# One PV pass moved ahead of the scores after six query groups, and query banks taken by halves

## The chip, the cores, the metric

One core of a Trainium2 chip. The time is the device time of one execution in microseconds (us). Each comparison runs two kernels on the same chip in alternating rounds; a ratio is the mean time of one kernel's fast runs over the mean of the other's fast runs of the same rounds, so it is not quite the ratio of the medians quoted beside it. The span of a profile is one profiled execution from its first to its last instruction, about 1.8 us less than its time.

## The reference, cut to what matters

```python
xn = layernorm(x)                                   # x: 2048 x 448
q  = (xn @ wq)          # 16 query heads of 256;  keys and values: 8 heads, the last 512 positions
p  = softmax(q @ k.T / 16)                          # per head 2048 x 512
s  = (p @ v, heads side by side) @ wo               # 2048 x 448
g  = silu((gelu(xn @ w_gate) * (xn @ w_up)) @ w_down)
out = x + s * g
```

## The kernel before

The kernel handles the feed-forward part first, then attention in 64 *steps*: 4 blocks of 512 rows times 16 query heads. Step m multiplies queries with keys (`s_mm`, "scores", eight passes of the matmul engine PE), takes exponentials on ScalarE (ACT), normalises on VectorE (DVE) and transposes the probabilities by DMA into `pT`. PV, the product with the values (`pv`, eight passes), follows two steps later (`LAG = 2`), so that PE has other work while a step's softmax and transpose run. Queries are made for up to eight steps at once, in query groups that start at steps 0, 4, 12, 18, 26, 34, 42, 50 and 58.

```python
def q_group(n, pairs, more_act=False):     # queries of two heads, into two pairs of banks
    ...
    group(units, 0, QC, True, True)        # 28 passes of 64 rows (two at a time: rows 0-63, rows 64-127)
    for i, b in enumerate(pairs):          # copied out by ScalarE (first half) and VectorE (second half)
        act(qT[:, s, 0, :], bank[b], ACT.Copy, (b_ps[b],), (b_qT[s][0],))
        K.op("dve", lambda v, s=s, b=b: v.tensor_copy(qT[:, s, 1, :], bank[b + 1]), ...)

def pv(m):
    h = m % Hq
    g, x = h // 2, m % NPT                 # g: key/value head, used by two query heads
    for e in range(2):
        b = BB[m % 2 * 2 + e]
        mms([(bank[b]..., va[:, g, j, e * P:(e + 1) * P], pT[:, x, ...], j == 0, j == NJ - 1)
             for j in range(NJ)], [b_va[g]] + b_pT[x], (b_ps[b],))     # NJ = 4, so 8 passes in all
        ...                                # copied out to oT

for m in range(NS):                        # cut to the order on PE
    if m in groups:
        for i in range(m, hi, 2):
            p = (i - m) // 2
            q_group(i, ((cur, nxt[::-1], (cur[1], nxt[1])) if three else (cur, nxt) * 2)[p], end)
            ...
            if m == Q0 + QS and p == 0:    # the third group, step 12
                for g in range(6, Hkv):
                    load_k(g)              # DMA transposes on the SP queue
                for g in range(5, Hkv):
                    load_v(g)              # plain loads on the same queue
    s_mm(m)
    ...
    if len(late) == LAG:
        pv(late.pop(0))
    ...
    late.append(m)
```

A bank is a stretch of the memory that PE writes its results to. `cur` and `nxt` are two bank pairs each: scores use the four banks of `cur` (`AB`), PV those of `nxt` (`BB`).

The softmax here doesn't subtract the row's maximum and nothing guards it: scores larger than these inputs give would overflow.

## Time and profile before

| | before |
|---|---|
| time, median of the first three runs | 540.66 us (540.63 to 542.68) |
| span of the profile | 540.2 us |
| PE busy | 533.2 us (99%) |
| all waits of PE that the profile names | 3.4 us |
| third query group's start to first score pass of step 13 | 13.00 us (187.16 to 200.16) |

Columns of the waits: the waiting engine and its line, what released it, then total us, times, longest. A row of the timeline: start in us, length in us, engine, line, operation, output<-inputs, shape, count; in brackets the idle time before it and its releaser. PEld is PE's weight load, L394 the helper through which nearly all matmuls go. Tiles tell the kinds: bank<-xnT,wq are queries, bank<-kT,qT scores, bank<-pT,va PV. The lines stand in the prediction. One more answer of the same trace, for the three value loads at step 12 (issue to landing):

```profile
L379 SPq DMA_DIRECT2D va<-in_A_v_cache_dram x3: 502/580/583, 192.1 to 193.3; - x3
...
DMA to landing us min/median/max: 6.3/6.3/7.5
```

The first of the three, key head 5, was issued at 192.12 and landed 6.26 us later, at 198.38.

### The profile page before, as it was taken

How to read it: one execution, taken by the hardware profiler on the slowest of the kernel's cores; microseconds unless marked ns; L12 is line 12 of the kernel's file. 1: busy time of each engine (PE TensorE's matmuls, PEld its weight loads, DVE VectorE, ACT ScalarE, POOL GpSimd, SP SyncE). 2: the span in 40 equal slices, each digit the busy share in tenths (PEclk: the TensorE clock that was granted, in tenths of full speed). 3: DMA queues.
4: the chain of work that ended last, by engine and by line, in shares of the span. 5: the costliest groups of instructions: out<-in, count | busy, mean ns of one | idle time of the engine just before them, and what ended most of it. 6: DMA issues, size and time to landing. Idle time of an engine off the chain costs nothing.

```text
span 540.2 us, 10920 instructions
## 1 busy us (share of the span) xinstructions
PE 533.2 (99%) x4155; PEld 310.6 (58%) x4180; DVE 383.6 (71%) x839; ACT 314.2 (58%) x782; POOL 39.7 (7%) x78
## 2 busy tenths in 40 slices
PE   9999999999999999999999999999999999999998
PEld 5556656459644444984444469544444884444487
DVE  6689886798767757934875786367667934776785
ACT  5466355873568768116866850488488106876820
POOL 1131120000000010003001000120000003001010
PEclk9999999999999999999999999999999999999999
DMA  9569173932598686302861860067448302872821
GB/s 296 123 187 108 53 126 87 282 70 60 112 171 138 156 190 147 59 1 82 167 141 50 152 137 1 18 156 139 96 106 146 72 1 69 164 157 73 149 66 35
DMA packets 171604, 61.38 MB, mean 114 GB/s; under 512 B 155104, under 2 KB 168416, under 8 KB 171552
## 3 DMA queue, kind: packets, MB, share of 16 engines
q1 hardware_dynamic: 167488, 51.30, 45.0%
q0 software_dynamic: 3008, 8.72, 6.9%
q8 instruction: 33, 0.54, 0.4%
q10 hardware_dynamic: 1056, 0.66, 0.4%
q14 instruction: 19, 0.16, 0.1%
HBM read 19.76 MB, written 3.67 MB: 43 GB/s over the span
## 4 chain that ended last, share of the span: by engine, by line
PE 87%; ACT 4%; DMA 4%; DVE 3%; issue 1%; SPq 1%; ACTq 0%; DVEq 0%
PE bank L394 86%; ACT p L830 4%; DMA pT<-pn 2%; DVE pn L837 2%; DMA va<-in_A_v_cache_dram 1%; PE bank L511 1%; DVE rden L834 1%; SPq L382 1%; PE bank L492 0%; DVE oTh L855 0%; ACT oTh L385 0%; DVE xnT L884 0%; DVE gl L424 0%; DVE xnT L388 0%; DVE epst L425 0%
## 5 line engine op out<-in xcount | busy, mean ns | idle before, releaser
L830 ACT ACTIVATE p<-bank 128x512 f32<-128x512 f32 x256 | 150.6, 596 | 28.9 <-DVE pn L837 26.5
L394 PE MATMUL bank<-pT,va 128*128 128x512 bf16 x512 | 120.9, 379 | 0.8 <-DMA pT<-pn 0.5
L394 PE MATMUL bank<-kT,qT 128*128 128x512 bf16 x487 | 117.8, 379 | 2.3 <-ACT qT L385 1.0
L837 DVE TENSOR_SCALAR pn<-p,rden 128x512 bf16<-128x512 f32 x256 | 112.9, 483 | 8.7 <-DMA pT<-pn 4.4
L394 PE MATMUL bank<-xnT,wq 64*128 64x512 bf16 x768 | 94.9, 376 | 0.0
L394 PEld LDWEIGHTS bank<-pT,va 128*128 128x128 bf16 x512 | 49.4, 98 | 62.5 <-DMA pT<-pn 3.2
L394 PEld LDWEIGHTS bank<-kT,qT 128*128 128x128 bf16 x512 | 49.3, 98 | 61.7 <-issue 3.4
L394 PE MATMUL bank<-xnT,wgu 64*128 64x512 bf16 (+2 forms) x768 | 83.9, 350 | 0.1
L385 ACT ACTIVATE qT<-bank 128x512 bf16<-128x512 f32 x76 | 44.1, 596 | 51.6 <-PE bank L394 50.0
L815 DVE CAST qT<-bank 128x512 bf16<-128x512 f32 x52 | 34.8, 690 | 49.4 <-PE bank L394 49.4
L394 PEld LDWEIGHTS bank<-xnT,wq 64*128 64x128 bf16 x768 | 36.7, 94 | 46.3 <-ACT p L830 1.7
L394 PEld LDWEIGHTS bank<-xnT,wgu 64*128 64x128 bf16 x768 | 37.6, 94 | 36.0 <-issue 0.5
L834 DVE RECIPROCAL rden<-rsum 128x2 f32<-128x2 f32 x128 | 21.1, 165 | 48.3 <-ACT p L830 48.2
L830 ACT ACTIVATION_READ_ACCUMULATOR p<-bank 128x1 f32 x256 | 51.6, 202 | 0.0
L394 PE MATMUL bank<-wt,sr 128*128 128x224 f16 x512 | 50.0, 259 | 0.0
L394 PEld LDWEIGHTS bank<-wt,sr 128*128 128x128 f16 x512 | 49.0, 98 | 0.4 <-ACT oTh L385 0.2
L385 ACT ACTIVATE gl<-bank 128x512 bf16<-128x512 f32 x56 | 33.0, 596 | 26.4 <-PE bank L394 22.1
L560 DVE TENSOR_TENSOR actTh<-bank,gl 128x512 f16<-128x512 f32 x56 | 37.4, 688 | 11.3 <-PE bank L394 5.8
L855 DVE TENSOR_SCALAR oTh<-bank 128x512 f16<-128x512 f32 x62 | 42.3, 683 | 0.0
L385 ACT ACTIVATE oTh<-bank 128x512 f16<-128x512 f32 x66 | 38.9, 590 | 3.8 <-PE bank L394 3.8
L394 PE MATMUL bank<-wt,oTh 128*128 128x224 f16 (+1 forms) x416 | 38.4, 252 | 0.0
L394 PEld LDWEIGHTS bank<-wt,oTh 128*128 128x128 f16 x416 | 37.2, 98 | 0.9
(77 smaller groups left out, 387.8 us busy)
## 6 DMA issues: line engine op xcount, KB each, us to landing
wtb<-in_A_wo_dram POOLq DMA_DIRECT2D x4, 896.0 KB, 10.8
wq<-in_A_wq_dram SPq DMA_DIRECT2D x2, 1536.0 KB, 7.9
va<-in_A_v_cache_dram SPq DMA_DIRECT2D x8, 256.0 KB, 6.3
pT<-pn SPq DMA_TRANSPOSE x128, 2.8
xr<-in_A_x_dram POOLq DMA_DIRECT2D x15, 112.0 KB, 2.3
wd<-in_B_w_down_dram SPq DMA_DIRECT2D x1, 1568.0 KB, 7.5
g<-g_all POOLq DMA_DIRECT2D x14, 112.0 KB, 2.3
out_dram<-xr POOLq DMA_DIRECT2D x12, 112.0 KB, 2.1
```

The lines of the kernel that those rows point to most:

```text
L382: K.op("sp", lambda e, o=o, i=i: e.dma_start_transpose(o, i), reads, writes, dma=True)
L385: K.op("act", lambda e, o=o, i=i: e.activation(o, i, func, scale=scale), reads, writes)
L394: ins = e.matmul(o, lhsT=l, rhs=r, start=st, stop=sp, skip_group_check=True)
L511: ins = e.matmul(bank[b][:, 0:w], lhsT=gl[:, 0, 0:P], rhs=gl[:, 0, 0:w], start=True, stop=True)
L560: K.op("dve", lambda e: e.tensor_tensor(actTh[:, c % 2, f, :], bank[b + 1], gl[:, s, :], ALU.mult), (b_ps[b + 1], b_gl[s]), (b_actT[c % 2] ...
L815: K.op("dve", lambda v, s=s, b=b: v.tensor_copy(qT[:, s, 1, :], bank[b + 1]), (b_ps[b + 1],), (b_qT[s][1],))
L830: K.op("act", lambda e, b=b, r=r, z=z: e.activation(p32[:, z, :], bank[b], ACT.Exp, scale=att_scale, accum_out=rsum[:, r:r + 1]), (b_ps[b] ...
L834: K.op("dve", lambda e, r=r: e.reciprocal(rden[:, r - 1:r + 1], rsum[:, r - 1:r + 1]), b_rsum[r - 1:r + 1], b_rden[r - 1:r + 1])
L837: K.op("dve", lambda e, r=r - 1 + t, z=(n - 1 + t) % NP32, y=y, t=t: e.tensor_scalar(pn[:, y, t, :], p32[:, z, :], rden[:, r:r + 1], None, ...
L855: K.op("dve", lambda v, i=i, b=b: v.tensor_scalar(oTh[:, i, :], bank[b], WS, None, op0=ALU.mult), (b_ps[b],), (b_oT[i],))
```

## The change

Its intent: after a query group, scores seem to wait for ScalarE's last query copies. One PV pass of the head two steps back is put between, as cover. PV's bank must be free by then, so in the groups of four query pairs (26, 34, 42, 50) the last two pairs each take one half of both bank sets (`cur[0], nxt[0]`, then `cur[1], nxt[1]`) instead of a whole set. The groups of three pairs (12, 58) keep their bank order. The early pass comes in six groups: steps 12, 26, 34, 42, 50 and 58.

```diff
-        def pv(m):
+        def pv(m, part=None):
...
-                     for j in range(NJ)], [b_va[g]] + b_pT[x], (b_ps[b],))
+                     for j in range(NJ) if part is None or (part == 0) == (e == j == 0)], [b_va[g]] + b_pT[x], (b_ps[b],))
+                if part == 0:
+                    break
...
         for m in range(NS):
+            split = m in groups and m not in (0, Q0, Hq + LAG)
...
-                    q_group(i, ((cur, nxt[::-1], (cur[1], nxt[1])) if three else (cur, nxt) * 2)[p], end)
+                    q_group(i, ((cur, nxt[::-1], (cur[1], nxt[1])) if three else (cur, nxt, (cur[0], nxt[0]), (cur[1], nxt[1])) if split else (cur, nxt) * 2)[p], end)
...
+            if split:
+                pv(late[0], 0)
             s_mm(m)
...
-                pv(late.pop(0))
+                pv(late.pop(0), 1 if split else None)
```

## The prediction

> **What bounds the kernel now.** I read the page first: the busy shares, the slices and the queues.
>
> ```profile
> span 540.2 us, 10920 instructions
> PE 533.2 (99%) x4155; PEld 310.6 (58%) x4180; DVE 383.6 (71%) x839; ACT 314.2 (58%) x782; POOL 39.7 (7%) x78
> PEclk9999999999999999999999999999999999999999
> ```
>
> The matmul engine (PE) is busy 99% of the span at the full clock in all 40 slices, and no other engine is above 71%. A busy PE is not a PE at its peak, though, so what can be won is in the spacing of its instructions. Next I read the waits of PE, the whole list:
>
> ```profile
> PE bank L511 <- DVE epst L425: 1.2, 1, 1.2
> PE bank L394 <- ACT qT L385: 1.0, 6, 0.2
> PE bank L394 <- issue: 0.5, 3, 0.2
> PE bank L394 <- DMA pT<-pn: 0.5, 2, 0.3
> PE bank L394 <- DMA va<-in_A_v_cache_dram: 0.2, 1, 0.2
> ```
>
> All its waits together come to 3.4 us. The line that the change seems aimed at is the second: six waits before the scores (bank<-kT,qT), put down to ScalarE's copy of the queries (ACT qT), 0.2 us each. Before believing it I looked at the timeline of PE and of its weight loads (PEld) around two of the places where queries (bank<-xnT,wq) give way to scores. The first is the third query group, ahead of head step 12:
>
> ```profile
> 194.94 1.46 PE L394 MATMUL bank<-xnT,wq 64*128 64x512 bf16 x12
> 196.56 1.67 PE L394 MATMUL bank<-kT,qT 128*128 128x512 bf16 x7 [0.16 <-issue]
> 198.42 1.90 PE L394 MATMUL bank<-pT,va 128*128 128x512 bf16 x8 [0.19 <-DMA va<-in_A_v_cache_dram]
> 200.16 1.89 PE L394 MATMUL bank<-kT,qT 128*128 128x512 bf16 x8
> ...
> 196.33 1.41 PEld L394 LDWEIGHTS bank<-kT,qT 128*128 128x128 bf16 x8 [0.42 <-issue]
> 198.42 1.41 PEld L394 LDWEIGHTS bank<-pT,va 128*128 128x128 bf16 x8 [0.69 <-DMA va<-in_A_v_cache_dram]
> ```
>
> The second is the group ahead of step 26, with the copies of the last query pair beside it:
>
> ```profile
> 289.72 1.46 PE L394 MATMUL bank<-xnT,wq 64*128 64x512 bf16 x12
> 290.57 1.25 ACT L385 ACTIVATE qT<-bank 128x512 bf16<-128x512 f32 x2 [1.78 <-PE bank L394]
> 291.11 1.41 PEld L394 LDWEIGHTS bank<-kT,qT 128*128 128x128 bf16 x8 [0.42 <-issue]
> 291.33 1.67 PE L394 MATMUL bank<-kT,qT 128*128 128x512 bf16 x7 [0.16 <-ACT qT L385]
> 292.85 1.89 PE L394 MATMUL bank<-pT,va 128*128 128x512 bf16 x8
> ```
>
> Three readings. (1) A 512-column pass takes 0.216 us start to start: eight take 200.16 - 198.42 = 1.73. Scores show "x7" although eight weights are loaded, and 292.85 - 291.33 = 1.52 is room for seven: the first score pass's record is missing. It began 0.216 earlier, at 196.34 and 291.12, with the weight loads. The 64-row query passes run in pairs, 0.216 a pair: twelve from 194.94 end their slots at 196.24, from 289.72 at 291.01. So the real hole before scores is about 0.10 us, not 0.16 plus. (2) The hole is the same where the profile names no releaser (step 12) and where it names ScalarE (step 26). The scores of step 26 use queries of the group's first pair and a bank of its third, copied more than 2 us before; the last pair's copies end at 291.82, after the scores began. So ScalarE did not end this wait. (3) At step 12 the PV pass had a real wait: it started 198.42 when its eight score passes had ended at 198.07, because the values of its key head had only then landed.
>
> **What the Trainium skill says.** "TensorEngine Tiling (Array Packing)", Key Properties: "Changing tiling mode (not just tile) drains the TensorE". "TensorE: Matmul & The Clock Gate", section "Step-by-step: what each phase is for", adds that a weight load is pulled ahead of running matmuls only where row groups don't conflict or it goes to the background buffer. The trace agrees: query passes use 64 rows (64*128), scores and PV 128 (128*128), every such switch costs about 0.10 us in either direction, and a 128-row to 128-row change (scores to PV at 292.85) costs none. The other direction:
>
> ```profile
> 277.09 1.89 PE L394 MATMUL bank<-pT,va 128*128 128x512 bf16 x8
> 278.92 0.82 PE L394 MATMUL bank<-xnT,wq 64*128 64x512 bf16 x6
> ```
>
> Eight passes from 277.09 end at 278.82; the next starts 278.92. The same page, Part 1 ("The HAM clock gate"), says that the clock falls to half after an idle window of some 3.4 us. No stall in this trace is long enough to show that.
>
> **The change part by part.** *Work.* Nothing is added or removed: order of instructions shows equal counts on DVE, ACT and SP in the same order. On PE, at the six groups before steps 12, 26, 34, 42, 50 and 58, one of the eight PV passes of the head two steps back moves ahead of the eight score passes; seven stay behind them. 16 x 0.216 = 3.45 us per step as before.
>
> *Banks by halves.* In the four-pair groups (26, 34, 42, 50) the third pair takes the front halves of both bank sets and the fourth the back halves, so the bank of the early PV pass was freed a pair ago. Scores 5 to 8 now use banks that the last pair filled. The first of these is finished three pairs (0.65 us) before the group's end; its copies start 0.44 before the end (290.57 against 291.01) and take 0.60 on ScalarE and 0.69 on VectorE, so they end at +0.16 and +0.25. Scores want those banks at 0.10 + 0.22 + 4 x 0.216 = +1.18 and +1.61. Margin 0.9 us: no wait. In the third pair the second bank half is wanted four slots (0.86) after the second pair's end and is free at +0.25. No wait either. Cost 0.
>
> *The hole.* The first 128-row pass after the queries is now PV instead of scores. It is still a switch from 64 to 128 rows with nothing loaded ahead. I expect the 0.10 us to stay in all six: gain 0.
>
> *Step 12.* Here the early PV pass belongs to step 10 and reads the values of key head 5. These are loaded by the SP queue behind the last transposes of the steps before and two key loads, all unchanged:
>
> ```profile
> 188.74 0.65 SPq L382
> 189.43 1.30 SPq L382
> 190.78 1.29 SPq L382
> 192.12 6.26 DMA va<-in_A_v_cache_dram
> 198.38 0.05 issue
> ```
>
> They land at 198.38 whatever PE does in between: every item of this chain is issued before PE leaves the query group. Before, the eight score passes (1.73 us) lay in that time and only 0.35 us was left over. After, PE meets the wait with the first pass at 196.24 and stands until 198.42. Then come one PV pass (to 198.64), eight scores (to 200.37) and seven PV (to 201.88). Before, this point was reached at 200.16. Cost +1.72 us. PE is the bound for the rest of the program, so nothing gives it back.
>
> *The later exponentials.* Scores come 0.22 us later at the other five groups, so softmax and its transposed tile (pT) for the first head do too, while the PV pass that needs them starts at the same time as before. By the landing times in the trace that slack is about 1.18 us at steps 26, 42 and 58 and falls to about 0.97. At 34 and 50, after a projection, it is only 0.04, but there ScalarE is held by a third query copy: its first exponential starts about 1.09 us after the scores' weights instead of 0.65, and 0.22 + 0.65 = 0.87 is still under that. Cost 0, at most 0.2 each.
>
> Sum: 0 + 0 + 1.72 + 0 = +1.7 us, 540.66 + 1.7 = 542.4.
>
> **The rivals.** *A: the intent works.* If the six waits are ScalarE's after all, or if PV weights can be loaded under 64-row passes where the query weights cannot, 0.10 us goes at each of five groups; with no wait at step 12 also there: 6 x 0.10 = 0.6, giving 540.1. Only the releaser column speaks for it; the equal hole at step 12 and at the switches the other way speak against. A mixed result (five holes closed, step 12 delayed) is 540.66 + 1.72 - 0.5 = 541.9. *B: the values land earlier.* Were the load tied to something the change moves, the loss would shrink. With no traffic moved I see nothing; the load took 6.26 us against 6.3 as the median of its kind, so it is not an outlier either. *C: the clock.* PE would stand for 2.2 us at step 12. That is under the 3.4 us of the page, but close; half a clock for one window would cost about 1.7 us more (an estimate from that page): 544.1. *D: late pT.* Waits of 0.3 us for a late transpose already occur at single heads (landings take 2.8 in the median, 4.7 at most); other phases may move a few, either way by some tenths.
>
> **Range and chances.** Step 12 is nearly certain in sign; its size depends on the landing, which may vary by a few tenths between runs. The three times of before are 540.63, 540.66 and 542.68, so one execution in three was 2 us longer by itself. I predict 542.4 us, 541.2 to 543.7 in 8 of 10. A 2% change is 10.8 us, over five times the largest effect I can name: faster 0.01, same 0.985, slower 0.005.
>
> **What would show it right or wrong.** Right: in the waits of PE the wait for va rises from 0.2 to about 2 us, sitting before one single PV pass ahead of step 12's scores, and step 13's scores start about 1.7 us later than 200.16. The small waits at the other five groups stay at about 0.16, now in front of a PV pass. Scores 5 to 8 after a group run at 0.216 spacing. PEclk stays 9 in the slice. Wrong: no long wait for va (the load lands before 196.3), five holes gone (rival A), score passes waiting for ScalarE or VectorE copies (my bank margin was wrong), or slowed passes after the stall (rival C).

## The result

The changed kernel took 542.33 us in the median of six runs (540.95 to 544.06), the kernel before 541.25 in the median of its six (540.63 to 542.68). The ratio is 1.0019, 95% interval 0.9997 to 1.0041: the same by the 2% measure, a mean of 1.0 us more, and by these runs alone not even clear of zero. Both spread over 2 to 3 us, so the traces must carry the argument. The page of the changed kernel and its list of PE's waits:

```profile
span 540.4 us, 10915 instructions
PE 533.0 (99%) x4155; PEld 311.2 (58%) x4180; DVE 383.5 (71%) x839; ACT 314.5 (58%) x782; POOL 39.7 (7%) x78
...
PEclk9999999999999999999999999999999999999999
```
```profile
PE bank L394 <- issue: 1.4, 2, 1.2
PE bank L511 <- DVE epst L425: 1.2, 1, 1.2
PE bank L492 <- DVE xn L467: 0.4, 1, 0.4
PE bank L394 <- ACT qT L385: 0.3, 2, 0.2
PE bank L394 <- DMA pT<-pn: 0.2, 1, 0.2
```

Six ACT qT waits became two. The two stand at steps 4 and 18, which the change leaves alone; the four that went stood at 26, 34, 42 and 50. The sum of that line fell by 0.7 us, yet nothing got shorter, as the groups below show. New is a wait of 1.2 us put down to "issue", that is to nothing the profile shows. PE's timeline says where, and the sequencer's own instructions (source line L153, the semaphore waits) say what:

```profile
194.40 1.46 PE L394 MATMUL bank<-xnT,wq 64*128 64x512 bf16 x12
197.11 0.38 PE L394 MATMUL bank<-pT,va 128*128 128x512 bf16 x1 [1.25 <-issue]
197.54 1.67 PE L394 MATMUL bank<-kT,qT 128*128 128x512 bf16 x7
199.05 1.67 PE L394 MATMUL bank<-pT,va 128*128 128x512 bf16 x7
200.56 1.89 PE L394 MATMUL bank<-kT,qT 128*128 128x512 bf16 x8
```
```profile
L153 PEldq EVENT_SEMAPHORE  x1: 2413/2413/2413, 194.6 to 194.6; - x1
```
```profile
L379 SPq DMA_DIRECT2D va<-in_A_v_cache_dram x3: 503/507/580, 191.6 to 192.8; - x3
...
DMA to landing us min/median/max: 5.4/5.5/7.0
```

The queries end their slots at 195.70. The PV pass starts at 197.11, alone, then eight scores (the first record is missing), then the other seven PV passes. PE's sequencer stood in one semaphore wait of 2413 ns from 194.64 to 197.06. The first value load was issued at 191.58 and took 5.44, so it landed at 197.02: the load ended the wait. In the kept trace that instruction names two semaphores, and the load is seen there directly: one belongs to the transposed tile and was last raised at 187.53, the other is the one that this load raises, last at 197.02. The profile names "issue" because the wait sits in an instruction of the sequencer ahead of the weight load and the weight load itself names another semaphore, satisfied at 195.86. "Perfetto Trace Analysis", section "Identifying Dependency Chains", says that an instruction which waits on several engines may have such EventSemaphore instructions ahead of it; this trace agrees, with that one instruction.

The start of the third group to step 13's scores took 200.56 - 186.62 = 13.94 us, 0.94 more than before. The spans differ by only 0.2. The rest is chance: waits of PV for late transposes elsewhere, counted from the weight loads, came to some 1.3 us in the trace of before and 0.6 in that of the change, at unrelated steps.

At the other five groups, here step 26:

```profile
290.33 1.46 PE L394 MATMUL bank<-xnT,wq 64*128 64x512 bf16 x12
291.73 0.39 PE L394 MATMUL bank<-pT,va 128*128 128x512 bf16 x1
292.17 1.67 PE L394 MATMUL bank<-kT,qT 128*128 128x512 bf16 x7
293.68 1.67 PE L394 MATMUL bank<-pT,va 128*128 128x512 bf16 x7
295.19 1.89 PE L394 MATMUL bank<-kT,qT 128*128 128x512 bf16 x8
```

Query slots end at 290.33 + 6 x 0.216 = 291.62 and the PV pass starts at 291.73: the hole of 0.10 us stands. From 291.73 to 295.19 lie 3.46 us, 16 passes and nothing else.

### The profile page after: what moved, and what is told of

Its sections match the earlier page's. It is cut to its first block, busy times and chain, and to the rows that moved or that the text cites. A ratio compares the mean times of both kernels' runs of the same rounds, so it can differ in the third digit from the quotient of the medians.

```text
span 540.4 us, 10915 instructions
## 1 busy us (share of the span) xinstructions
PE 533.0 (99%) x4155; PEld 311.2 (58%) x4180; DVE 383.5 (71%) x839; ACT 314.5 (58%) x782; POOL 39.7 (7%) x78
## 4 chain that ended last, share of the span: by engine, by line
PE 97%; DMA 1%; issue 1%; DVE 1%; ACT 0%
PE bank L394 96%; DMA pT<-pn 1%; DMA x<-in_A_x_dram 0%; ACT p L830 0%; DVE stats L441 0%; PE bank L492 0%; DVE pn L837 0%; ACT oTh L385 0%; DVE xn L467 0%; DVE mv L444 0%; PE bank L511 0%; DVE xnT L887 0%; DVE xnT L388 0%; DVE rden L834 0%; DVE rstd L461 0%
```

## The experiments

My theory: the change costs only at step 12, where PE must stand until key head 5's values land; everything else is worth nothing, and the hole is the switch from 64 to 128 rows. Rival A: the waits were ScalarE's, and five groups gain 0.10 us each. Further rivals: the split pass or the bank order costs by itself; the clock falls.

One table for all traces. "Landing" is that of key head 5's values, "step 13" the first score pass of step 13, both in us after the third group's start (for the changed kernel, 197.02 - 186.62 and 200.56 - 186.62). In some expectations the end point is the weight load of that pass, 0.21 earlier (0.43 at half clock).

| kernel | landing | step 13 | ratio to before (interval) |
|---|---|---|---|
| before | 11.22 | 13.00 | |
| changed | 10.40 | 13.94 | 1.0019 (0.9997 to 1.0041) |
| e1: step 12 only | 10.45 | 13.98 | 1.0038 (1.0023 to 1.0054) |
| e2: the other five only | 10.76 | 12.64 | 1.0001 (0.9986 to 1.0016) |
| e3: bank halves only | 11.03 | 12.81 | one look |
| e7: 128 query rows at full height | 10.01 | 12.63 | one look |
| e6: all eight PV passes first at step 12 | 10.34 | 13.89 | one look |
| e4: changed, values 5 first | 5.43 | 12.63 | 1.0000 (0.9984 to 1.0015) |
| e5: before, values 5 first | 5.43 | 12.63 | 0.9992 (0.9978 to 1.0006) |
| e10: the same again | 5.47 | 12.63 | 0.9992 (0.9977 to 1.0006) |
| e8: changed, values 5 last | 12.88 | 18.11 | one look |
| e9: before, values 5 last | 13.36 | 16.73 | one look |

### e1: step 12 only

```diff
-            split = m in groups and m not in (0, Q0, Hq + LAG)
+            split = m == Q0 + QS
```

> The early PV pass at step 12 only; the other five groups as in the kernel before. My theory (the whole cost is the values of key head 5 landing late at step 12): a wait of 1.2 to 2.2 us before one PV pass ahead of step 12's scores; from the start of the third query group to the start of step 13's scores some 13.9 to 14.8 us, against 13.0 in the kernel before and 13.9 in the changed one; mean time 0.9 to 1.7 us over the kernel before, that is a ratio of 1.002 to 1.003. Rival (each split PV pass costs or gains something by itself): a sixth of the change's difference, 0.2 us at most, and no long wait.

Measured: 543.62 us in the median against 541.61; the means of 543.71 and 541.80 differ by 1.9 us; the interval of the ratio spans 1.2 to 2.9 us. PE's timeline:

```profile
194.74 1.46 PE L394 MATMUL bank<-xnT,wq 64*128 64x512 bf16 x12
197.49 0.38 PE L394 MATMUL bank<-pT,va 128*128 128x512 bf16 x1 [1.30 <-issue]
197.71 1.89 PE L394 MATMUL bank<-kT,qT 128*128 128x512 bf16 x8
```

The same wait in front of the same pass. This one group alone costs no less than the whole change: its mean is even higher, with overlapping intervals. The mean lies a little above the 0.9 to 1.7 expected, the trace (13.98 against 13.00) inside.

### e2: the other five groups only

```diff
-            split = m in groups and m not in (0, Q0, Hq + LAG)
+            split = m in groups and m not in (0, Q0, Q0 + QS, Hq + LAG)
```

> The early PV pass and the banks by halves at the other five groups, step 12 as in the kernel before. My theory: the start of the query group to the second step's scores is as long as before at all five groups (the 0.10 us hole stays, now before the PV pass), third group 13.0 us as before; time equal to the kernel before, ratio 1.000 within 0.001. Rival A (the intent works, the six waits were ScalarE's): 0.10 us less at each of the five groups, 0.5 us in all, ratio 0.999.

Measured: ratio 1.0001. From group start to the second step's scores, counted by weight loads, the groups at 26, 34, 42 and 50 took 15.45 us and the last 12.42, as in the kernel before to 0.01 us. The cover buys nothing: rival A falls. Here step 12 did not wait at all (12.64): the values landed as the scores ended.

```profile
194.42 1.46 PE L394 MATMUL bank<-xnT,wq 64*128 64x512 bf16 x12
195.81 1.90 PE L394 MATMUL bank<-kT,qT 128*128 128x512 bf16 x8
197.55 1.89 PE L394 MATMUL bank<-pT,va 128*128 128x512 bf16 x8
```

The 13.00 of the kernel before thus holds 0.36 us of wait that not every execution has.

### e3: bank halves without the early pass

```diff
             if split:
-                pv(late[0], 0)
+                pass
...
-                pv(late.pop(0), 1 if split else None)
+                pv(late.pop(0))
```

> The banks by halves in the four-pair groups without any early PV pass (scores come first as in the kernel before). My theory: all groups as long as before (15.45, 12.42 in the last, the third 12.4 to 12.8 by its landing), since scores 5 to 8 find their banks free 0.7 us ahead. Rival (the bank order needs the early pass as cover): scores 5 to 8 wait for copies, groups 26, 34, 42 and 50 are longer by 0.1 us or more.

Measured: all groups 15.45 and 12.42 again; the bank order is free, with or without cover. This trace says more. Scores come first here, as in the kernel before:

```profile
289.22 1.46 PE L394 MATMUL bank<-xnT,wq 64*128 64x512 bf16 x12
290.61 1.90 PE L394 MATMUL bank<-kT,qT 128*128 128x512 bf16 x8
```

The hole is 290.61 - (289.22 + 6 x 0.216) = 0.10 us, as before. But now all eight score passes are recorded, and the list of PE's waits has no line for ACT qT any more:

```profile
PE bank L511 <- DVE epst L425: 1.2, 1, 1.2
PE bank L394 <- DMA pT<-pn: 0.2, 1, 0.2
```

So the six waits of 0.2 us were there because the first score record was missing in that trace and the hole looked 0.2 us longer than it was. The wait for ScalarE that the change set out to cover was not there; what is there is the hole of 0.10 us. (The traces of before and of the changed kernel each lack the first score record of the same 25 steps, 487 of 512; the other ten have all 512.)

### e7: what the hole is

In the kernel before, the last query pair of each group does its first 128 rows of the contraction at full height, at the end: four passes of 128 rows in place of four slots of two 64-row passes.

```diff
-                        if k == NK and ph == 1:
+                        if k == NK and ph == 1 or k == 0 and full:
...
+            for (b, w, wr, cols, reads, rreads, xts) in units if full else ():
+                lst = [(bank[b + j][:, lo:hi], w(j, 0), xnT[:, 0, cols], False, stop) for j in range(2)]
+                o = mms(lst, reads + [y for x in xts for y in x], b_ps[b:b + 2], [last_row[b][0]])
```

> The kernel before, where in the last pair of every query group the first 128 rows of the contraction are done in full-height passes (128 rows), four of them, moved to the end of the group; the same work and the same number of slots. If the 0.10 us hole is the switch from 64 to 128 rows: the hole moves ahead of these four query passes and the scores follow them at 0.216 us without a hole; group lengths unchanged within 0.05 us (15.45 and 12.4). If the hole is a wait of the scores for copies by ScalarE, it stays right before the scores and perhaps grows, as these copies now start up to 0.2 us later.

Measured at step 26 (PE, then its weight loads):

```profile
288.89 2.00 PE L394 MATMUL bank<-xnT,wq 64*128 64x512 bf16 x12
290.72 1.89 PE L394 MATMUL bank<-kT,qT 128*128 128x512 bf16 x8
```
```profile
289.11 0.31 PEld L394 LDWEIGHTS bank<-xnT,wq 64*128 64x128 bf16 x4
289.85 0.55 PEld L394 LDWEIGHTS bank<-xnT,wq 128*128 128x128 bf16 x4 [0.42 <-PE bank L394]
290.51 1.39 PEld L394 LDWEIGHTS bank<-kT,qT 128*128 128x128 bf16 x7
```

The twelve query passes are eight of 64 rows (four slots, to 289.75) and four of 128. The first full-height one starts with its weights at 289.85, so 0.10 us later; four of them end at 290.72, exactly when the scores start, their weights loaded 0.21 ahead. The hole went with the switch of row mode although these are query passes that need no copy, and the scores behind them, with the copies due even later, have none. The group is as long as before (278.52 to step 27's scores at 294.18, 15.66; before 278.92 to 294.57, 15.65). It is the switch; how much of it is drain and how much the uncovered weight load stays open.

### e4 and e5: values of key head 5 first

```diff
-                        for g in range(6, Hkv):
-                            load_k(g)
-                        for g in range(5, Hkv):
-                            load_v(g)
+                        load_v(5)
+                        for g in range(6, Hkv):
+                            load_k(g)
+                        for g in range(6, Hkv):
+                            load_v(g)
```

On the changed kernel (e4) and on the kernel before (e5, and again as e10):

> The changed kernel with the values of key head 5 loaded first in the block of loads at step 12, ahead of two transposing key loads, so that they are issued some 2.7 us earlier. My theory: they land about 194 to 195.5 us, before the queries end at about 196; no wait before the early PV pass beyond the 0.10 us hole; third group to step 13's scores 12.6 us; time equal to or up to 0.4 us under the kernel before. If the pass itself or the bank order were what costs, the time would stay about 1 us over the kernel before. Risk for mine: the keys of head 6 now come 0.6 us later and could make step 12's scores wait; the slack there is over 3 us.

> The kernel before with that same earlier load and nothing else: a candidate that beats both. My theory: the 0.36 us wait before PV at step 12 goes, so third group to step 13's scores 12.6 us, 0.3 to 0.4 us under the kernel before, ratio 0.9993, which the runs' own scatter of about 1 us may hide. Equal to the run with the change and the earlier load within 0.1 us in that stretch, since the early pass is worth nothing by itself; rival A says that the one with the change is 0.5 us faster.

> The same kernel as in the run with the earlier load and without the change, timed again, because its interval there (0.9978 to 1.0006) left open whether it beats the kernel before. From the traces the wait before step 12's PV in the kernel before was 0.37 us in one execution and none in another, so the mean gain should be 0.1 to 0.4 us, a ratio of 0.9993 to 0.9998: the interval will most likely still hold 1.

Measured for e4 (PE):

```profile
194.51 1.46 PE L394 MATMUL bank<-xnT,wq 64*128 64x512 bf16 x12
195.90 0.39 PE L394 MATMUL bank<-pT,va 128*128 128x512 bf16 x1
196.13 1.89 PE L394 MATMUL bank<-kT,qT 128*128 128x512 bf16 x8
197.85 1.67 PE L394 MATMUL bank<-pT,va 128*128 128x512 bf16 x7
```

The values landed at 192.16, earlier than I had expected, 3.15 us after their issue instead of 5.0 to 6.3 behind the two key loads. The early pass starts after the 0.10 us hole, and with the change left whole its cost is gone: ratio 1.0000. The keys of heads 6 and 7, now issued 0.6 us later, delayed nothing; but head 6's landed at 194.77, only 1.4 us before step 12's scores, where I had expected a slack of over 3. With the early load, change and no change are alike in this stretch (12.63 both).

e5 and e10 are the candidate to beat both kernels. Medians 541.15 and 541.05 against 541.61 and 541.52 of before; the ratio is 0.9992 both times, the intervals 0.9978 to 1.0006 and 0.9977 to 1.0006. The two are no independent confirmation of each other: eleven of the twelve runs of before are the same. The wait is gone in both traces, a gain of up to 0.4 us in the executions that have it, but that the time is lower is not shown.

### e6: eight passes first instead of one

```diff
+            if m == Q0 + QS:
+                pv(late.pop(0))
             s_mm(m)
```

> The kernel before, with all eight PV passes of step 10 ahead of step 12's scores instead of one, at this group only. My theory (PE waits for the landing and then has 16 passes left, whichever come first): third group to step 13's scores is the landing (counted from the group's start) plus 3.33 us, as with one early pass, so 13.6 to 14.2 us; dose does not matter. Rival (each early pass costs by itself): eight times the cost of one, over 16 us.

Measured (steps 12 and 13 follow each other in the second line, eight passes each, so step 13 starts at 198.94 + 8 x 0.216 = 200.67):

```profile
197.22 1.89 PE L394 MATMUL bank<-pT,va 128*128 128x512 bf16 x8 [1.19 <-issue]
198.94 3.19 PE L394 MATMUL bank<-kT,qT 128*128 128x512 bf16 x14
```

That is 13.89 at a landing of 10.34, against 13.94 at 10.40 with one pass. The dose does not matter; the place in the order does.

### e8 and e9: values of key head 5 last

```diff
-                        for g in range(5, Hkv):
+                        for g in (6, 7, 5):
                             load_v(g)
```

On the changed kernel (e8) and on the kernel before (e9):

> The changed kernel with the values of key head 5 loaded last of the three instead of first. Third loads landed 12.7 to 13.6 us after the group's start so far. My theory: third group to step 13's scores is that landing plus 3.33 us, 16.0 to 16.9 us, against 13.7 in the changed kernel. The wait is then about 4 us, longer than the idle window of 3.4 us in the Trainium skill's page TensorE: Matmul & The Clock Gate: if that reached PE here, passes after the wait would take 0.43 us for up to 3.4 us, 1.7 us more; if not, 0.216 at once.

> The kernel before with the values of key head 5 loaded last of the three. My theory: third group to step 13's scores is the landing plus 1.57 us, 14.3 to 15.2 us, that is 8 passes or 1.73 us less than in the changed kernel at the same landing; the wait stands before PV and after the scores and is about 2.3 us.

Measured: the lengths from landing alone would be 12.88 + 3.54 = 16.42 and 13.36 + 1.78 = 15.14 (3.54 and 1.78 are 13.94 - 10.40 and 13.00 - 11.22 of the table). They are 18.11 and 16.73, 1.6 to 1.7 us more. PE in e8 (two lines), then in e9:

```profile
199.82 0.38 PE L394 MATMUL bank<-pT,va 128*128 128x512 bf16 x1 [3.73 <-issue]
200.04 3.38 PE L394 MATMUL bank<-kT,qT 128*128 128x512 bf16 x8
...
195.82 1.90 PE L394 MATMUL bank<-kT,qT 128*128 128x512 bf16 x8
200.05 3.53 PE L394 MATMUL bank<-pT,va 128*128 128x512 bf16 x8 [2.33 <-DMA va<-in_A_v_cache_dram]
```

The clock had fallen. Busy time by stretch, in e8 and then in e9 (start:end, length, busy us and count of PE, PEld, DVE, ACT and POOL, then the granted clock, DMA share and GB/s):

```profile
196.00:200.00 4.00, 0.27 (x3) 0.13 (x2) 0.82 (x2) 0.68 (x2) 0.00 (x0) 1.00 0.53 144
200.00:203.40 3.40, 3.40 (x10) 1.25 (x9) 0.90 (x3) 2.06 (x6) 0.00 (x0) 0.54 0.00 0
203.40:207.00 3.60, 3.60 (x18) 1.59 (x16) 1.85 (x6) 2.63 (x8) 0.00 (x0) 0.96 0.47 107
```
```profile
196.00:200.00 4.00, 1.72 (x8) 0.59 (x6) 2.43 (x7) 2.99 (x9) 0.00 (x0) 1.00 0.51 144
200.00:203.40 3.40, 3.35 (x9) 1.20 (x10) 0.28 (x1) 0.60 (x1) 0.00 (x0) 0.52 0.68 154
203.40:207.00 3.60, 3.60 (x18) 1.67 (x17) 1.83 (x5) 2.66 (x9) 0.00 (x0) 0.98 0.00 0
```

After standing some 3.9 us (e8) and 2.5 us (e9: from the end of the scores at 197.55 to 200.05), passes start every 0.43 us for 3.4 us. That loses half of 3.4, the missing 1.7. For e8 I had named this as one of two outcomes; for e9 I had not expected it, and its 2.5 us is shorter than the window I had relied on. The clock records of the kept traces suggest why: in e9 and e8 they give full clock for 194.56 us, half for 3.41, full for 341.33, that is 57, 1 and 100 times 3.413, so the clock steps seem to fall on a grid. The grid's stretch that ended with the fall in e9, 196.75 to 200.16, was not idle throughout: score passes ran in it until 197.55, and PV from 200.05.

## Why the prediction was right or wrong

The time came out as predicted: 542.4 against a median of 542.33, inside the range. That the two agree to 0.1 us is luck: I had added 1.7 us to 540.66, but the kernel before had 541.25 in its six runs, and the change cost about 1.0 (interval of the ratio: -0.2 to 2.2). A base too low and a cost too high cancelled. Step by step:

- **Work, banks, hole: right.** Groups 26 to 58 kept their length to 0.01 us (changed kernel, e2, e3); scores 5 to 8 followed at 0.216. e7 shows that the hole belongs to the row switch, and e3 that the six named waits were a missing record. The line of six that I took for the target holds two waits (steps 4 and 18) that the change does not touch.
- **Step 12, mechanism: right.** One pass moved ahead of the scores makes PE wait for a load that the scores had hidden. e1 has the cost alone, e2 has none, e4 takes the wait away and the cost with it, and e6 shows that dose is irrelevant. The sign I had named, about 2 us in the line for va, did not come: the wait was 1.25 us and stood under "issue".
- **Step 12, size: too sure.** The failed step is "They land at 198.38 whatever PE does in between". The landing is no fixed moment. I had allowed it "a few tenths" and called 6.26 us no outlier because the median of its kind was 6.3; the same answer gave 4.0 and 7.5 as the extremes of the eight loads. In the traces where key head 5 comes first of the three value loads but behind the keys, it fell between 10.0 and 11.2 us after the group's start (11.22 in the one I had read, 10.40 after, 10.01 in e7). By the table's numbers the change ends this stretch at the landing plus 3.54, the kernel before at the landing plus 1.78 or at 12.63, whichever is later. So the cost is 1.76 at a landing of 11.2 and 1.3 at 10.4; between the two profiles, with two different landings, it was 0.94 instead of my 1.72. Timed means say 1.0 for the change and 1.9 for e1; their intervals overlap.
- **Later exponentials: right.** The transposed tile's slack at steps 26, 42 and 58 measured 0.96 to 0.97 us (predicted 0.97), and the waits at 34 and 50 did not grow.
- **Rivals.** A fell (e2, e7). B, that the values land earlier, is what happened. It looks like scatter and not the change's doing: unchanged orders gave 10.01 to 11.22, and the second key load ahead of the values differs already (8.95 us after the group's start in before, 8.24 in e7, 8.50 in the changed kernel), before the queries end at 9.1. C did not occur in the change, with a stall of 1.4 us. My reason for its absence was weak, though: e9 lost its clock after 2.5 us, and I had predicted a stall of 2.2. D is real: waits for late transposes sum to between 0 and about 1.3 us in the traces and move with every run.

## What to carry to other kernels

Before moving an operation earlier, list all that it waits for, loads too: one pass of 0.2 us brought a wait of 1.4 us forward, and it would have been free behind an earlier load. A wait of equal length at many places, put down to different releasers or to something long done, can be the engine's own cost or a missing record; check the counts and place the same kind of switch somewhere else before covering it. Treat a DMA's landing as a spread, not as a moment, and take it from several traces.

## What the Trainium skill lacked or had wrong

- "TensorEngine Tiling (Array Packing)", Key Properties, says that a change of tiling mode drains the engine, without a size. Here each switch between 64 and 128 rows cost about 0.10 us, in either direction, and moved with the switch (e7).
- "TensorE: Matmul & The Clock Gate", Part 1, gives one idle window of about 3.4 us for the fall to half clock. Here 2.5 us of standing were enough (e9, granted clock 0.52 in the next 3.4 us), in a stretch of 3.41 us that also held some 0.9 us of passes; 1.4 us were not (changed kernel, clock 9 in all slices). A stall need not fill the window's length; where between the two the limit lies is open.
- "Perfetto Trace Analysis" tells of semaphore instructions ahead of an instruction, but not that their own records can hold the wait: here 1.25 us stood under "issue", and the sequencer's instruction of 2413 ns, with the semaphores that it names, showed the load.
- No page that I read tells of matmul records that are missing in a regular way: the traces of before and of the changed kernel lack the first score pass of the same 25 steps (487 records of 512, with all 512 weight loads), 16 of them in before and 22 in the changed kernel behind other full-height passes, not behind a row switch; e3 has all 512. One missing record of 0.216 us made a hole of 0.10 us look like a wait of 0.16.
